# Attention stage of a fused kernel: conversion steps moved between GpSimd and VectorE, expert weights loaded over more steps

## The chip, the cores and the metric

One core of a Trainium2 chip runs the whole program. The metric is the device time of one execution in microseconds; lower is better.

## The reference

Three layers follow one another: a linear attention with decay, a soft mixture of experts, and an ELU feed-forward. Cut to what matters:

```python
for t in range(S):                                   # attention: B=4, H=8, S=768, D=48
    cur = einsum('bhd,bhe->bhde', u * k[t], v[t])
    y[t] = einsum('bhd,bhde->bhe', r[t], state + cur)
    state = w * state + einsum('bhd,bhe->bhde', k[t], v[t])
logits = x @ phi                                     # soft MoE: 3072 tokens, 384 wide, 8 experts x 4 slots
d = softmax over tokens;  c = softmax over slots
slot_out[e] = relu((d.T @ x)[e] @ w1[e]) @ w2[e]     # w1: 384 x 1024, w2: 1024 x 384
x = c @ slot_out
h = x @ w_in                                         # ELU layer, 384 -> 2048 -> 384
out = where(h > 0, h, exp(min(h, 0)) - 1) @ w_out
```

The weights `w_in` and `w_out` of the last layer arrive as 64-bit floating-point numbers, and the kernel converts them to 32 bits with integer and float instructions.

## The kernel before, in words

The program has three stages: attention (to about 175 us), the experts, and the feed-forward. The change touches attention alone.

**Attention.** The 3072 tokens are cut into 24 chunks of 128 (4 batches of 6 chunks). One loop, `for s in range(-2, NCH)`, runs over them as a pipeline: step s finishes chunk s, computes the scores of chunk s + 1 and transposes r and k of chunk s + 2. Every engine executes its instructions in the order in which this loop writes them, so the order of the calls in the loop body is the schedule. In one step VectorE has: `t` (state, line 582), `km` (k times decay, line 517), `x` (output of the chunk, line 635), two `am` (causal masks on the scores, line 559), `rT` (scaling of the transposed r, line 532) and `qd` (r x k, line 529). TensorE has the state update, the rows of the output, the scores, and the transposes: `ps_r` of r, `ps_k` of k. The transposes share two PSUM buffers, so `ps_k` waits until `rT` has read `ps_r`. ScalarE copies `ps_k` to `kT` (line 527) and the state to `qb` (line 589). GpSimd multiplies the state by its decay (`qc`, line 583) and v by the bonus (`bv`, line 601). Between these stand, through `extra()`, the instructions of the experts' softmax over groups of three chunks (`al`, `nmx`, `et`, `pall`, `zr`): each three steps bring each of them once.

**Conversion.** 20 pieces of 128 x 384 numbers of `w_in` and `w_out` are converted during attention, one in each of the steps 0 to 19. `wide(j, f)` performs one part of it on piece j; all work in the tile `scr`:

- `wide_a`, ScalarE, lines 313 and 314: absolute value of the high word; the low word as a float.
- `wide_b1`, line 317, the clamp: limits the absolute value to the range of exponents. In attention it is given `nc.gpsimd`, so GpSimd does it.
- `wide_b2`, VectorE, line 322, the shift: shift left by 3 and a bit mask.
- `wide_b3`, VectorE, line 328, the merge: sign and top bits of the high word are put in.
- `wide_c`, VectorE, line 333, the mask: keeps sign and exponent.
- `wide_d`, GpSimd, lines 336 and 337, the product of the low word and the scale, and the sum; it is done one step later, for piece s - 1.

The raw data of three pieces and the working words of two fit in `scr`, so `wide_load(s + 2)` waits for `wide_d` of piece s - 1. The second stage of this conversion, in the feed-forward, calls the same functions with the clamp on VectorE.

**Loads.** SyncE issues all large loads in order: r, k and v of the chunks ahead, a piece for the conversion, and the experts' weights (`load_we`, 1.5 MB a set, 16 sets) into ten buffers, one of which holds `scr` until the last piece is done. Sets 0 to 8 are issued at the ends of steps by a rule that spreads them, set 9 when `scr` is free, set 10 in two halves in steps 21 and 22.

Of the kernel before, what the change touches and what calls it, by code (L numbers as in the profile page):

```python
# [236 lines left out]
def kernel(  # L237
# [14 lines left out]
    nc = tc.nc  # L252
# [25 lines left out]
    NWE = 10  # L278
    we_p = main.enter_context(tc.tile_pool(name="we_p", bufs=NWE, side="right"))
# [33 lines left out]
        nc.scalar.activation(out=a.bitcast(F32), in_=raw[:, :, 1].bitcast(F32), func=ACTF.Abs)  # L313
        nc.scalar.activation(out=l.bitcast(F32), in_=l.bitcast(U32), func=ACTF.Copy, scale=2.0 ** -52)

    def wide_b1(raw, a, eng=None):
        (eng or nc.vector).tensor_scalar(  # L317
            out=a.bitcast(F32), in0=a.bitcast(F32), scalar1=EXP_LO, scalar2=EXP_HI, op0=ALU.max, op1=ALU.min
        )

# [31 lines left out]
    def load_we(i, pool, part=None):  # L352
        if part in (None, 0):
            t = pool.tile([128, 2 * HW], F32, tag="we", name=f"we{i}")
            we[i] = [t[:, :HW], t[:, HW:]]
        for h in range(2) if part is None else [part]:
            load_half(i, h)

    def load_half(i, h):
        n = FE if i < E else DM  # L360
        src = (w1[i] if i < E else w2[i - E]).rearrange("(k p) f -> p k f", p=128)
        at = 0
        while at < HW:
            k, c = divmod(HW * h + at, n)
            m = min(HW - at, n - c)
            if c == 0 and m == n:
                m = (HW - at) // n
                nc.sync.dma_start(
                    out=we[i][h][:, at:at + n * m].rearrange("p (k f) -> p k f", k=m), in_=src[:, k:k + m]
                )  # L370
                at += n * m
            else:
                nc.sync.dma_start(out=we[i][h][:, at:at + m], in_=src[:, k, c:c + m])
                at += m
# [22 lines left out]
    with ExitStack() as actx:  # L397
# [22 lines left out]
        def warm(n):  # L420
            ps = pt_p.tile([128, 4, 128], F32, tag="pt", name="warm")
            for i in range(n):
                nc.tensor.matmul(out=ps[:, i % 4, :], lhsT=ident, rhs=ident, start=True, stop=True)
# [95 lines left out]
        def turn(i, n):  # L519
            ps = pt_p.tile([128, HP, 128], F32, tag="pt", name=f"ps_{'rk'[i]}")  # L520
            for p in range(HP):
                nc.tensor.transpose(  # L522
                    out=ps[:, p, :], in_=(km if i else rp[n % 2])[:, 2 * p:2 * p + 2, :].rearrange("p a d -> p (a d)"),
                    identity=ident,
                )
            if i:
                nc.scalar.copy(out=kT, in_=ps)  # L527
                qd[n] = at2.tile([128, HP, 128], F32, tag="qd", name="qd", bufs=1)
                nc.vector.tensor_tensor(out=qd[n], in0=rT[n], in1=ps, op=ALU.mult)
            else:  # L530
                rT[n] = at2.tile([128, HP, 128], F32, tag="rT", name="rT", bufs=2)
                nc.vector.tensor_tensor(out=rT[n], in0=ps, in1=vt, op=ALU.mult)  # L532
# [58 lines left out]
        def bonus_b(n):  # L591
            bt = misc.pop(n)
            pb = pm_p.tile([128, 128], F32, tag="pm", name="ps_c")
            nc.tensor.transpose(out=pb, in_=bt, identity=ident)
            bs = at2.tile([128, H], F32, tag="bs", name="bs", bufs=1)
            nc.scalar.copy(
                out=bs.rearrange("p (a b) -> p a b", b=2),
                in_=pb.rearrange("p (a b) -> p a b", b=32)[:, :, 0:2],
            )
            bv = at2.tile([128, H, D], F32, tag="bv", name="bv", bufs=1)  # L600
            nc.gpsimd.tensor_tensor(out=bv, in0=vd[n], in1=bs.unsqueeze(2).to_broadcast([128, H, D]), op=ALU.mult)  # L601
            bsb[n] = bv
# [79 lines left out]
        def slots_b(j):  # L682
            el, ps, nj = lg[j], lg[j, 0], nmx[:, j:j + 1]
            nc.scalar.activation(out=el[:, 0, :], in_=ps[:96], func=ACTF.Exp, bias=nj, accum_out=zz[:, j:j + 1])
            if j:
                nc.scalar.activation(out=wt[j], in_=nmx[:, j - 1:j], func=ACTF.Exp, scale=-1.0, bias=nj)
# [54 lines left out]
        def last_part(j):  # L741
            slots_a(j, False)
            slots_b(j)
            combine_a()
            warm(4)
            extra()
            slots_c(j, (0,))
            warm(2)
            slots_d(j, (0,))
            slots_g(j)  # L750
            combine_c()
            slots_e(j)
            slots_f(j)
            slots_c(j, (1,))
            warm(2)
            combine_b()
            slots_d(j, (1,))
# [25 lines left out]
        NP = -(-NW // PW)  # L783
# [29 lines left out]
        def wide(j, f):  # L813
            if 0 <= j < NP:
                raw, a = piece(j)
                if f is wide_b1:
                    f(raw, a, nc.gpsimd)
                    return
                if f is not wide_d:
                    f(raw, a)  # L820
                    return
                merged = []
                for o, at, i, c, p, m in spans(j):
                    if merged and merged[-1][0] == o:
                        merged[-1][3] += m
                    else:
                        merged.append([o, at, p, m])
                for o, at, p, m in merged:
                    wide_d(raw[:, at:at + m, :], a[:, at:at + m], (wov if o else wiv)[:, p:p + m])
# [18 lines left out]
        nwe = 0  # L848
        extras = [lambda: None] * 7 + [flags_a, lambda: None, lambda: None, flags_b, lambda: None, flags_c, flags_d]

        def extra():
            if extras:
                extras.pop(0)()
# [3 lines left out]
        for s in range(-2, NCH):  # L857
            now, nxt, ahead = s >= 0, 0 <= s + 1 < NCH, s + 2 < NCH
            last = s == NCH - 1
            if nxt:  # L860
                update(s + 1)
            wide(s, wide_a)
            wide(s, wide_b1)
            if last:
                extra()
                extra()
                extra()
                logits(GS - 1, 0, G - 1)
            else:
                extra()  # L870
            if s > 0 and s % G == 0:
                extras += part(s // G - 1)
            if s == -2:
                tables_b()
            if nxt:
                state(s + 1)
            if ahead:
                scale(s + 2)
            if 2 <= s + 4 < NCH:
                load_k(s + 4)  # L880
            if 2 <= s + 3 < NCH:
                load_v(s + 3)
            if s < 1:
                wide_load(s + 2)
            if now:
                for p in range(HP):
                    rows_a(s, p)
                rows_b(s)
                wide(s, wide_b2)
                wide(s - 1, wide_d)  # L890
                if s >= 1 and s + 2 < NP:
                    wide_load(s + 2)
            if nxt:
                for p in range(HP):
                    scores(s + 1, p)
                causal(s + 1)
                bonus_a(s + 1)
                bonus_c(s + 1)
            if not last:
                extra()  # L900
            if ahead:
                turn(0, s + 2)
            if 2 <= s + 4 < NCH:
                load_r(s + 4)
            if nxt:
                for p in range(HP):
                    before(s + 1, p)
            if now:
                x_T(s)
            if last:  # L910
                logits(GS - 1, G - 1, G)
            if nxt:
                bonus_b(s + 1)
            wide(s, wide_b3)
            wide(s, wide_c)
            if ahead:
                turn(1, s + 2)
            if nxt:
                state_b(s + 1)
            if s == NCH - 2:  # L920
                warm(3)
            extra()
            if s >= 2 and (s - 2) * (NWE - 1) // (NP - 3) >= nwe and nwe < NWE - 1:
                load_we(nwe, we_p)
                nwe += 1
            if s == NP:
                assert nwe == NWE - 1
                load_we(nwe, we_p)
                nwe += 1
            if s >= NCH - 3 and not last:  # L930
                h = s - NCH + 3
                (rk_ctx, early)[h].close()
                pool = w2ctx.enter_context(tc.tile_pool(name=f"we2a{h}", bufs=1, side="right", reuse_waits="tile"))
                we.setdefault(NWE, []).append(pool.tile([128, HW], F32, name=f"we2a{h}"))
                load_half(NWE, h)
                nwe = NWE + h
        last_part(GS - 1)
        assert not extras

# [464 lines left out]
```

## Time and profile before

| | us |
|---|---|
| three runs | 466.58, 467.81, 467.82 |
| median | 467.81 |
| the profiled execution | 467.28 |
| its span, first to last instruction | 465.5 |
| TensorE busy | 416.9 (90% of the span) |
| VectorE busy | 369.6 (79%) |
| ScalarE busy | 268.5 (58%) |
| GpSimd busy | 186.3 (40%) |

The time of an execution holds a little more than its span. Busy times are sums over the whole span, in which the three stages have different limits; the attention stage is read from its own stretch.

### The profile page before, as it was taken

Reading aid. Unit: us, or ns where it says so; the run is one execution under the profiler, and the core shown is the slowest. Engines: PE = TensorE matmul, PEld = TensorE weight load, DVE = VectorE, ACT = ScalarE, POOL = GpSimd, SP = SyncE. Lnnn points to the kernel's source line nnn. Section 1 sums busy time; section 2 is a strip of 40 time slices with the busy share of each in tenths; the row PEclk is TensorE's granted clock in tenths of the full one; section 3 lists DMA queues with packets and bytes.
Section 4 is the critical chain, followed back from the end, with each engine's and each line's share of the span. In section 5 each row is a group of like instructions: output and inputs, shape, how many; then the busy total and the mean of one; then the engine's idle time right before and its main releaser. Section 6 shows DMA issues by size and latency. Waiting matters only on the chain.

```text
span 465.5 us, 9991 instructions
## 1 busy us (share of the span) xinstructions
PE 416.9 (90%) x4009; PEld 365.4 (78%) x4009; DVE 369.6 (79%) x553; ACT 268.5 (58%) x487; POOL 186.3 (40%) x185
## 2 busy tenths in 40 slices
PE   7888788798879898995999899989999999999995
PEld 6777677676768774443899789969998989999994
DVE  4798889898988854454887999996999987787851
ACT  2444254345445332485677787867868686866740
POOL 2385667777777613200000245331234304324440
PEclk9999899999999999998899999999999999999999
DMA  9959989999999858850000111211111001111112
GB/s 127 214 124 273 232 211 252 259 281 261 277 233 244 228 200 271 294 182 0 2 1 0 34 35 35 67 36 35 34 35 34 1 0 51 36 52 68 70 70 73
DMA packets 97575, 57.41 MB, mean 123 GB/s; under 512 B 77808, under 2 KB 89328, under 8 KB 97520
## 3 DMA queue, kind: packets, MB, share of 16 engines
q1 hardware_dynamic: 96704, 56.64, 45.2%
q8 instruction: 33, 0.54, 0.5%
q14 instruction: 22, 0.18, 0.1%
q10 hardware_dynamic: 816, 0.05, 0.1%
HBM read 51.96 MB, written 4.72 MB: 122 GB/s over the span
## 4 chain that ended last, share of the span: by engine, by line
PE 50%; DVE 16%; POOL 13%; ACT 10%; issue 8%; DMA 3%; POOLq 0%; DVEq 0%; ACTq 0%; SPq 0%
PE fo L1256 12%; PE fo L1257 11%; PE fo L1259 11%; POOL scr L317 5%; PE fh L1211 3%; DVE ex L1230 3%; DVE ex L1225 3%; DMA scr<-in_moe_w_out_dram 2%; POOL scr L336 2%; PE ph L1011 2%; POOL bv L601 2%; DVE am L559 2%; ACT scr L313 1%; PE ps_a L554 1%; ACT th L1219 1%
## 5 line engine op out<-in xcount | busy, mean ns | idle before, releaser
L1256 PE MATMUL fo<-wh,gh 128*128 128x384 f32 x384 | 132.3, 344 | 7.0 <-ACT gh L1238 3.7
L1257 PE MATMUL fo<-wl,gh 128*128 128x384 f32 x384 | 130.7, 340 | 0.0
L1259 PE MATMUL fo<-wh,gl 128*128 128x384 f32 x384 | 122.2, 340 | 0.0
L1256 PEld LDWEIGHTS fo<-wh,gh 128*128 128x128 f32 x384 | 72.9, 190 | 14.0 <-ACT acc L1193 6.5
L1225 DVE SCALAR_TENSOR_TENSOR ex<-ex,th 128x1024 f32<-128x1024 f32 (+1 forms) x52 | 62.1, 1195 | 23.3 <-ACT ex L1222 23.1
L336 POOL TENSOR_TENSOR cv<-raw,cv 128x384 f32<-128x384 f32 x12 | 19.8, 1652 | 138.7 <-DVE cv L333 66.4
L1241 DVE TENSOR_TENSOR gl<-ex,gh 128x1024 fp32r<-128x1024 f32 (+1 forms) x52 | 72.0, 1385 | 3.5 <-ACT gh L1238 3.0
L1219 ACT ACTIVATE th<-fh 128x1024 f32<-128x1024 f32 (+1 forms) x53 | 50.3, 949 | 42.4 <-PE fh L1211 42.4
L1257 PEld LDWEIGHTS fo<-wl,gh 128*128 128x128 f32 x384 | 72.8, 190 | 1.9
L1259 PEld LDWEIGHTS fo<-wh,gl 128*128 128x128 f32 x384 | 72.2, 190 | 0.0
L1230 DVE SCALAR_TENSOR_TENSOR ex<-ex,fh 128x1024 f32<-128x1024 f32 (+1 forms) x52 | 58.8, 1131 | 0.1
L1222 ACT ACTIVATE ex<-fh 128x1024 f32<-128x1024 f32 (+1 forms) x53 | 50.3, 949 | 9.5 <-DVE gl L1241 9.4
L1238 ACT CAST gh<-ex 128x1024 fp32r<-128x1024 f32 (+1 forms) x52 | 51.5, 991 | 5.4 <-DVE ex L1230 4.2
L1198 POOL TENSOR_TENSOR acc<-os,acc 128x384 f32<-128x384 f32 x20 | 29.0, 1482 | 49.7 <-ACT os L1197 49.7
L317 POOL TENSOR_SCALAR scr<-scr 128x384 f32<-128x384 f32 x20 | 30.8, 1538 | 35.7 <-ACT scr L313 35.7
L522 PE MATMUL ps_k<-ident,km 128*128 128x128 f32 x96 | 15.9, 290 | 23.5 <-DVE rT L532 22.2
L646 ACT COPY xT<-ps_x 128x384 f32<-128x384 f32 x24 | 11.5, 479 | 38.6 <-PE ps_x L644 38.6
L1211 PE MATMUL fh<-cT,mst 128*128 128x512 f32 x96 | 31.0, 404 | 2.8 <-DVE ex L1230 2.8
L522 PEld LDWEIGHTS ps_k<-ident,km 128*128 128x128 f32 x96 | 10.4, 143 | 28.4 <-DVE rT L532 26.7
L527 ACT COPY kT<-ps_k 128x512 f32<-128x512 f32 x24 | 14.1, 587 | 30.4 <-PE ps_k L522 30.2
L559 DVE TENSOR_TENSOR am<-ps_a,mask 128x512 f32<-128x512 f32 x48 | 30.7, 678 | 0.9 <-PE ps_a L554 0.9
L554 PE MATMUL ps_a<-rT,kT 64*128 64x128 f32 x384 | 29.0, 292 | 0.6 <-DVE rT L532 0.6
(160 smaller groups left out, 729.0 us busy)
## 6 DMA issues: line engine op xcount, KB each, us to landing
we<-in_moe_w_dram SPq DMA_DIRECT2D x14, 768.0 KB, 7.6
we<-in_moe_w_dram SPq DMA_DIRECT2D x16, 512.0 KB, 6.4
rp<-in_r_dram SPq DMA_DIRECT2D x24, 192.0 KB, 4.7
rk<-in_k_dram SPq DMA_DIRECT2D x24, 192.0 KB, 4.9
vd<-in_v_dram SPq DMA_DIRECT2D x24, 192.0 KB, 5.2
out_dram<-acc SPq DMA_DIRECT2D x24, 192.0 KB, 1.9
we<-in_moe_w_dram SPq DMA_DIRECT2D x16, 256.0 KB, 6.0
scr<-in_moe_w_out_dram SPq DMA_DIRECT2D x10, 384.0 KB, 5.1
```

Source lines behind the costliest of these rows:

```text
L317: (eng or nc.vector).tensor_scalar(out=a.bitcast(F32), in0=a.bitcast(F32), scalar1=EXP_LO, scalar2=EXP_HI, op0=ALU.max, op1=ALU.min)
L559: nc.vector.tensor_tensor(out=am[n, a], in0=aps[a], in1=mask.unsqueeze(1).to_broadcast([128, HP, 128]), op=ALU.mult)
L1211: nc.tensor.matmul(out=ph[n][:, i, :], lhsT=mst[(f + i) // 8][:, 128 * ((f + i) % 8):128 * ((f + i) % 8) + 128], rhs=cT[:, TB * blk:TB * b ...
L1219: nc.scalar.activation(out=th[n][:, s], in_=ph[n][:, s], func=ACTF.Tanh, scale=0.5)
L1222: nc.scalar.activation(out=ex[n][:, s], in_=ph[n][:, s], func=ACTF.Exp)
L1225: nc.vector.scalar_tensor_tensor(out=ex[n][:, s], in0=ex[n][:, s], scalar=1.0, in1=th[n][:, s], op0=ALU.add, op1=ALU.mult)
L1230: nc.vector.scalar_tensor_tensor(out=ex[n][:, s], in0=ex[n][:, s], scalar=0.0, in1=ph[n][:, s], op0=ALU.min, op1=ALU.max)
L1238: nc.scalar.copy(out=gh[n][:, s], in_=ex[n][:, s])
L1241: nc.vector.tensor_tensor(out=gl[n][:, s], in0=ex[n][:, s], in1=gh[n][:, s].bitcast(F32), op=ALU.subtract)
L1256: nc.tensor.matmul(out=o, lhsT=gh[n][:, i, s], rhs=wh, start=(f == first), stop=False)
L1257: nc.tensor.matmul(out=o, lhsT=gh[n][:, i, s], rhs=wl, start=False, stop=False)
L1259: nc.tensor.matmul(out=o, lhsT=gl[n][:, i, s], rhs=wh, start=False, stop=(f == final))
```

## The change

1. The clamp is no longer called right behind `wide_a` for GpSimd. It stands on VectorE behind `rows_b` (that is, behind `x` and ahead of `am`), where the shift stood.
2. The shift stands behind `bonus_b` and ahead of `turn(1, ...)`, that is on VectorE between `rT` and `qd`.
3. Merge and mask stand behind `turn(1, ...)`, that is behind `qd`.
4. Sets 0 to 8 of the experts' weights are spread by `(s - 2) * 9 // 20` instead of `// 17`: they are issued at the ends of steps 2, 5, 7, 9, 11, 14, 16, 18 and 20 instead of 2, 4, 6, 8, 10, 12, 14, 16 and 18; set 9 in step 21 instead of 20.

```diff
-    def wide_b1(raw, a, eng=None):
-        (eng or nc.vector).tensor_scalar(
+    def wide_b1(raw, a):
+        nc.vector.tensor_scalar(
...
         def wide(j, f):
             if 0 <= j < NP:
                 raw, a = piece(j)
-                if f is wide_b1:
-                    f(raw, a, nc.gpsimd)
-                    return
...
             wide(s, wide_a)
-            wide(s, wide_b1)
...
                 rows_b(s)
-                wide(s, wide_b2)
+                wide(s, wide_b1)
                 wide(s - 1, wide_d)
...
             if nxt:
                 bonus_b(s + 1)
+            wide(s, wide_b2)
+            if ahead:
+                turn(1, s + 2)
             wide(s, wide_b3)
             wide(s, wide_c)
-            if ahead:
-                turn(1, s + 2)
...
-            if s >= 2 and (s - 2) * (NWE - 1) // (NP - 3) >= nwe and nwe < NWE - 1:
+            if s >= 2 and (s - 2) * (NWE - 1) // NP >= nwe and nwe < NWE - 1:
                 load_we(nwe, we_p)
                 nwe += 1
-            if s == NP:
-                assert nwe == NWE - 1
-                load_we(nwe, we_p)
-                nwe += 1
+            if s == NP + 1:
+                load_we(NWE - 1, we_p)
```

VectorE before, one step from rT to rT (`scr` is the conversion's tile; lines 322, 328 and 333 are shift, merge and mask):

```order
L532 TENSOR_TENSOR rT<-ps_r,vt 128x512
L328 SCALAR_TENSOR_TENSOR scr<-scr 128x384
L333 TENSOR_SCALAR scr<-scr 128x384
L529 TENSOR_TENSOR qd<-rT,ps_k 128x512
L669 TENSOR_REDUCE al<-ps_l 96x1
L670 TENSOR_SCALAR nmx<-al,nmx 96x1
L582 TENSOR_TENSOR t_149<-qc,pu 128x192
L517 TENSOR_TENSOR km<-rk_835,wk 128x8x48
L635 TENSOR_TENSOR x<-py,bv 128x384
L322 TENSOR_SCALAR scr<-scr 128x384
L559 TENSOR_TENSOR am<-ps_a,mask 128x512 x2
L532 TENSOR_TENSOR rT<-ps_r,vt 128x512
```

Merge and mask (lines 328 and 333) stand together between rT and qd, the shift (line 322) alone ahead of am.

VectorE in the same step of the change:

```order
L532 TENSOR_TENSOR rT<-ps_r,vt 128x512
L322 TENSOR_SCALAR scr<-scr 128x384
L529 TENSOR_TENSOR qd<-rT,ps_k 128x512
L328 SCALAR_TENSOR_TENSOR scr<-scr 128x384
L333 TENSOR_SCALAR scr<-scr 128x384
L669 TENSOR_REDUCE al<-ps_l 96x1
L670 TENSOR_SCALAR nmx<-al,nmx 96x1
L582 TENSOR_TENSOR t_149<-qc,pu 128x192
L517 TENSOR_TENSOR km<-rk_829,wk 128x8x48
L635 TENSOR_TENSOR x<-py,bv 128x384
L317 TENSOR_SCALAR scr<-scr 128x384
L559 TENSOR_TENSOR am<-ps_a,mask 128x512 x2
```

Between rT and qd there is now one conversion instruction (the shift) instead of two, behind qd there are two instead of none, and ahead of am the clamp (line 317) has the shift's place.

GpSimd before, one step and the start of the next:

```order
L317 TENSOR_SCALAR scr<-scr 128x384
L583 TENSOR_TENSOR qc<-t_149,w_141 128x192
L336 TENSOR_TENSOR scr<-scr 128x384
L337 TENSOR_TENSOR win<-scr 128x384
L601 TENSOR_TENSOR bv<-vd,bs 128x384
L317 TENSOR_SCALAR scr<-scr 128x384
```

Each step begins with the clamp (line 317), ahead of qc.

GpSimd in the change, the same place:

```order
L583 TENSOR_TENSOR qc<-t_149,w_141 128x192
L336 TENSOR_TENSOR scr<-scr 128x384
L337 TENSOR_TENSOR win<-scr 128x384
L601 TENSOR_TENSOR bv<-vd,bs 128x384
L583 TENSOR_TENSOR qc<-t_149,w_141 128x192
```

The clamp at the head of each step is gone, and qc follows bv directly.

## Rows read from the trace of the kernel before

The view by stretches (rows 1) has these columns: stretch, its length, busy us (and instructions) of TensorE's matmuls, its weight loads, VectorE, ScalarE and GpSimd; then granted clock, DMA share and GB/s. The views in order of time have the start in us, the duration in us, engine, line, operation, output and inputs, shapes, and in brackets the idle time before and what ended it.

**Rows 1.** Busy us of each engine, TensorE's granted clock, DMA share, GB/s, by stretches.
```profile
41.40:152.60 111.20, 92.88 (x1578) 78.43 (x1578) 97.75 (x184) 51.86 (x152) 79.25 (x77) 0.98 1.00 253
161.00:168.00 7.00, 7.00 (x140) 6.40 (x137) 5.45 (x13) 2.77 (x9) 1.52 (x2) 1.00 1.06 380
168.00:175.00 7.00, 5.83 (x88) 4.68 (x85) 3.01 (x7) 1.69 (x7) 0.83 (x1) 1.00 0.17 60
49.00:56.00 7.00, 6.11 (x87) 5.07 (x88) 5.81 (x12) 2.00 (x5) 4.66 (x5) 0.76 0.79 215
```

**Rows 2.** VectorE in order of time (start, us): the first and last rT.
```profile
41.40 0.68 DVE L532 TENSOR_TENSOR rT<-ps_r,vt 128x512 f32<-128x512 f32 x1
...
152.62 0.67 DVE L532 TENSOR_TENSOR rT<-ps_r,vt 128x512 f32<-128x512 f32 x1
```

**Rows 3.** VectorE in order of time, one step (in brackets: idle before, released by).
```profile
111.45 0.68 DVE L532 TENSOR_TENSOR rT<-ps_r,vt 128x512 f32<-128x512 f32 x1
112.05 0.66 DVE L328 SCALAR_TENSOR_TENSOR scr<-scr 128x384 int32<-128x384 int32 x1
112.75 0.87 DVE L333 TENSOR_SCALAR scr<-scr 128x384 int32<-128x384 int32 x1
113.55 0.69 DVE L529 TENSOR_TENSOR qd<-rT,ps_k 128x512 f32<-128x512 f32 x1
114.16 0.25 DVE L700 COPY et<-ps_e 128x96 f32<-128x96 f32 x1
114.32 0.35 DVE L582 TENSOR_TENSOR t<-qc,pu 128x192 f32<-128x192 f32 x1
...
115.05 0.55 DVE L635 TENSOR_TENSOR x<-py,bv 128x384 f32<-128x384 f32 x1
116.52 0.66 DVE L322 TENSOR_SCALAR scr<-scr 128x384 int32<-128x384 int32 x1 [0.91 <-POOL scr L317]
117.09 1.28 DVE L559 TENSOR_TENSOR am<-ps_a,mask 128x512 f32<-128x512 f32 x2
118.29 0.68 DVE L532 TENSOR_TENSOR rT<-ps_r,vt 128x512 f32<-128x512 f32 x1
```

**Rows 4.** GpSimd (POOL) in order of time, the same step.
```profile
112.26 1.14 POOL L601 TENSOR_TENSOR bv<-vd,bs 128x384 f32<-128x384 f32 x1
114.79 1.69 POOL L317 TENSOR_SCALAR scr<-scr 128x384 f32<-128x384 f32 x1 [1.39 <-ACT scr L313]
116.45 0.50 POOL L583 TENSOR_TENSOR qc<-t,w 128x192 f32<-128x192 f32 x1
```

**Rows 5.** VectorE in order of time, qd in a step without a piece.
```profile
160.72 0.69 DVE L529 TENSOR_TENSOR qd<-rT,ps_k 128x512 f32<-128x512 f32 x1 [1.72 <-ACT kT L527]
```

**Rows 6.** Lines 317 and 333: ns min/median/max, first and last start.
```profile
L317 DVE TENSOR_SCALAR cv<-cv x12: 347/348/356, 252.3 to 364.4; 128x384 f32<-128x384 f32 x12
L333 DVE TENSOR_SCALAR scr<-scr x20: 360/869/872, 21.4 to 153.9; 128x384 int32<-128x384 int32 x20
```

**Rows 7.** GpSimd and VectorE in order of time, near 89.3 us.
```profile
89.24 1.02 POOL L336 TENSOR_TENSOR scr<-scr 128x384 f32<-128x384 f32 x1
...
89.31 1.17 DVE L322 TENSOR_SCALAR scr<-scr 128x384 int32<-128x384 int32 x1 [1.31 <-POOL scr L317]
```

**Rows 8.** VectorE and GpSimd in order of time, the step behind the last piece.
```profile
155.49 0.35 DVE L582 TENSOR_TENSOR t<-qc,pu 128x192 f32<-128x192 f32 x1
...
155.98 0.69 POOL L583 TENSOR_TENSOR qc<-t,w 128x192 f32<-128x192 f32 x1 [1.42 <-ACT c_sb L702]
...
156.63 1.02 POOL L336 TENSOR_TENSOR scr<-scr 128x384 f32<-128x384 f32 x1
156.72 0.69 DVE L559 TENSOR_TENSOR am<-ps_a,mask 128x512 f32<-128x512 f32 x1
```

**Rows 9.** VectorE in order of time: softmax instructions ahead of t in another step.
```profile
121.00 0.61 DVE L720 SCALAR_TENSOR_TENSOR pall<-pall,al,ps_s 96x384 f32<-96x384 f32 x1
...
121.65 0.34 DVE L582 TENSOR_TENSOR t<-qc,pu 128x192 f32<-128x192 f32 x1
```

More of the change, by code (lines that the diff above doesn't have):

```diff
@@ L936 @@
                 nwe = NWE + h
+        assert nwe == NWE + 1
         last_part(GS - 1)
```

## Prediction, made before the changed kernel was run

> **What bounds the kernel now.** I read the busy time by stretches first, then VectorE's and GpSimd's instructions of one step in order of time, then the places where one of them waits.
>
> Of the 111.2 us in which 16 of the 20 pieces are converted, VectorE is busy for 97.75, TensorE for 92.88, GpSimd for 79.25 [rows 1]. No engine is full, so the stretch is a ring of waits. One turn of it is one step, from r's scaling (rT) to the next rT: 41.40 to 152.62 for 16 steps [rows 2], 111.22 us, 6.95 us a step.
>
> A step [rows 3, 4]: rT starts at 111.45. It lets TensorE transpose k, ScalarE copies the result (kT) and VectorE's r x k (qd) waits for that copy: where nothing lies between, qd sat idle for 1.72 us and the releaser is kT [rows 5]. In a step with a piece qd starts 2.10 us after rT (113.55 - 111.45), and that time is filled exactly by the merge (line 328) and the mask (line 333). Then ScalarE takes the absolute value of the next piece, GpSimd's clamp waits for it and runs from 114.79 for 1.69 us, and VectorE's shift (line 322) waits 0.91 us for the clamp [rows 3, 4]. Behind the shift stand the two causal masks (am) and the next rT. So the ring is rT, k's transpose, kT, ScalarE, clamp, shift, am, rT, and the slow clamp is on it.
>
> **The change part by part.**
>
> *The clamp leaves GpSimd.* It goes from the ring, with the 0.91 us wait: a gain. GpSimd then has only qc, the product and the sum (lines 336 and 337) and bv in a step.
>
> *The clamp on VectorE, between x and am.* Undisturbed this instruction takes 0.35 us on VectorE: the second stage has twelve of them, 347 to 356 ns [rows 6]. But the one-input integer instructions on VectorE that run beside GpSimd here do not keep their 0.36 us (the mask's minimum); the mask's median is 0.87 [rows 6]. The row that explains it: GpSimd's product starts at 89.24 and lasts 1.02 us, VectorE's shift starts 0.07 us later and lasts 1.17, until 0.22 us after the product's end [rows 7]. The mask does the same beside bv: bv ends at 113.40, the mask at 113.62 [rows 3, 4]. So such an instruction that finds a GpSimd product running waits for its end.
>
> The Trainium skill says why, in "SBUF — State Buffer", section "SBUF: two separate sides": VectorE in a two-port mode and GpSimd share a port pair, whoever starts first holds it for the whole instruction, and the other blocks. By that rule too the clamp costs either its bare time or the rest of a GpSimd instruction, and who starts first decides; the 1.17 us row agrees.
>
> Who starts first? In the step where the last piece's products run and no clamp is left [rows 8], t starts at 155.49, qc on GpSimd at 155.98 and the product at 156.63, that is 1.14 us behind t; the instruction behind x on VectorE (there am) starts at 156.72, 1.23 us behind t. The clamp will stand in that place. It comes 0.09 us after the product, nearly the 0.07 us of the blocked shift [rows 7]. So I take 1.17 us and not 0.35. Successors start some 0.08 us before an instruction ends (rT lasts 0.68, the merge starts 0.60 behind it [rows 3]), so the clamp delays am by 1.09 us blocked, 0.30 us free. These are the two ends.
>
> *The shift into the gap behind rT.* It takes 0.36 us free, 0.66 as it stood [rows 3], or until 0.22 us behind bv's end; all of it lies in the 2.10 us before qd. Cost nothing; if bv came 1 us later than now, qd would slip.
>
> *Merge and mask behind qd.* They leave a gap which now stays partly empty and come onto VectorE's line: 0.60 us for the merge (0.70 beside bv as it stands [rows 3], the upper end; bv will be over) and 0.30 for the mask. The mask's bounds are 0.36 and 0.87 us [rows 6]; it comes some 3.3 us after rT, and bv, which began 0.81 us after rT and took 1.14 [rows 3, 4], is through by then, so the lower. Who waits for the mask: the product, which stands behind qc anyway.
>
> *The sum of a step.* rT to qd 2.10, qd to the next 0.61, merge 0.60, mask 0.30; then the softmax instructions e; t to clamp 1.23; clamp 1.09; the two am 1.20 (118.29 - 117.09) [rows 3]: 7.13 + e. e is 0.16 in one step of three (et, 114.16 to 114.32 [rows 3]), 0.65 in the next (pall to t, 121.00 to 121.65 [rows 9]), and I put the third kind between, 0.40, an estimate; mean 0.40. That is 7.53 us against 6.95. VectorE alone is then the ring: it has no wait but the one for kT. TensorE, busy 92.88 of 111.2 us at these steps, has room.
>
> Sixteen steps: +0.58 x 16 = +9.3; three of them have no t, a 0.26 us shorter line, -0.8. Of the four steps before, three at +0.5; the first has no product on GpSimd yet, its clamp is free and the wait is gone, -0.6. The step behind the last piece has merge and mask on the line, no clamp: +0.5. Sum +9.9.
>
> *Experts' weights over 20 steps.* Each set is loaded up to three steps later, the last at step 21 instead of 20. Loads get thinner in the piece steps, where 253 GB/s flow; no wait of the ring names a load there, so I count no gain. At the end about one set (1.5 MB) more lies behind step 20: at 380 GB/s some 4.1 us [rows 1], an estimate. The 7 us after it move 60 GB/s at a share of 0.17, so 5.8 us are free. Zero; if that cover were gone, up to 4 us.
>
> 467.28 us (the profiled execution; its span is 465.5) + 9.9 = **477.2 us**. That execution lies 0.53 us under the median of the three runs, 467.81, closer than the sum is sure.
>
> **The rivals.**
>
> *The clamp comes first (faster).* If it starts before the product, it costs 0.30 us and the product waits. A step is then 6.34 + 0.40 = 6.74: 13 steps at -0.21 are -2.7. In the three without t the products run earlier, the clamp meets the second one, and they stay near 7.27: +0.9. Three earlier steps -0.6, the first -0.6, the last +0.5: -2.5, **464.8 us**. For it: the margin is 0.09 us, read off starts, and the instruction in that place, an am, takes no part in the blocking [rows 8]. Against it: the shift was blocked at 0.07 [rows 7]. The point that decides is whether the product starts less than 1.23 us behind t. By the rule of the Trainium skill's "SBUF — State Buffer" (the section above) nothing but this order decides, and the one case at hand, [rows 7], went as it says.
>
> *In some steps first, in some not (no change).* Each free clamp saves 0.79 us, so some 11 or 12 of the 16 to 17 blocked ones must come free to end within the bound of no change: about 468. The steps repeat to 0.02 us in the trace, which speaks against a mixture.
>
> *TensorE's clock falls (slower still).* TensorE's work per step stays, the step grows, so it idles more. Once in the kernel before, after the long step that began at 41.40, the granted clock fell: 0.76 over 49 to 56 us, part of it at 1.2 GHz instead of 2.4 [rows 1]. That is 7 x 0.24 = 1.7 us of full-speed time for one fall. Three more falls not covered by its idle time give +5: **482 us**. Against it: other long steps went by at 1.00, the 111.2 us hold 0.98 in the mean.
>
> **How the numbers follow.** Forecast 477.2 us with a chance of 0.63 (474 to 480, from the bounds of merge, mask and e); clamp first 464.8, 0.21; mixture 468, 0.07; clock 482, 0.09. The range from 464.0 to 482.0 takes in the forecast, the mixture, over half of the fast rival and about half of the clock rival; the likeliest case alone is 474 to 480. Within 0.3% (1.4 us, about what a measurement of this kernel can tell from no change) only part of the mixture and the edge of the fast rival lie: 0.06. Faster 0.22, slower 0.72.
>
> **What would show it.** Right: line 317 on VectorE at about 1.17 us, ending 0.2 us behind the product of line 336; qd with some 1 us idle time released by kT in every piece step; the wait of the shift for the clamp gone; GpSimd's busy time down by about 30 us; rT to rT 7.2 to 7.8 us. Wrong: a clamp of 0.35 us in most steps (then the fast rival), a shift that ends after kT (then qd slips and the step is longer than the sum), or steps short of 6.9 us whose end a load or TensorE sets. Attention's end should move by all of the difference, and the stages behind it by nothing.

## The result, and the profile after

| | before | change |
|---|---|---|
| runs (4 each), us | 466.57 to 467.82 | 460.32 to 462.08 |
| median, us | 467.19 | 460.93 |
| ratio, 95% interval | | 0.9872 [0.9844, 0.9899] |
| profiled execution, us | 467.28 | 460.49 |

The change is faster by 6.3 us. The prediction said slower, 477.2 us, and its range began at 464. The page of the changed kernel, parts 1 and 4 (busy us, share of the span, instructions; shares of the chain that ended last):

```profile
span 458.8 us, 10035 instructions
...
PE 416.3 (91%) x4009; PEld 360.9 (79%) x4009; DVE 369.1 (80%) x573; ACT 267.9 (58%) x487; POOL 156.6 (34%) x165
...
PE 57%; DVE 22%; ACT 10%; issue 8%; DMA 2%; POOL 1%; SPq 0%; DVEq 0%; ACTq 0%; POOLq 0%
```

Part 4 of before:

```profile
PE 50%; DVE 16%; POOL 13%; ACT 10%; issue 8%; DMA 3%; POOLq 0%; DVEq 0%; ACTq 0%; SPq 0%
```

GpSimd lost 29.7 us of work and has almost left the chain, where VectorE and TensorE took its place. The busy times of TensorE, VectorE and ScalarE are those of before within 1 us. The view by stretches (columns as in [rows 1]) for the same 16 steps, whose first and last rT [rows 2] now start at 38.50 and 146.50:

```profile
38.50:146.50 108.00, 94.81 (x1578) 77.08 (x1578) 98.29 (x200) 51.32 (x150) 56.92 (x61) 1.00 0.98 250
```

108.0 us, against 111.2 of before [rows 1] and 119.7 of the forecast (13 steps of 7.53, three of 7.27). Attention's start gained too: 29.3 us from the first rT to 38.50, where before took 32.2. VectorE of the change in order of time, one step and the next up to qd (columns as in [rows 3]):

```profile
98.20 0.68 DVE L532 TENSOR_TENSOR rT<-ps_r,vt 128x512 f32<-128x512 f32 x1
98.80 0.47 DVE L322 TENSOR_SCALAR scr<-scr 128x384 int32<-128x384 int32 x1
100.30 0.69 DVE L529 TENSOR_TENSOR qd<-rT,ps_k 128x512 f32<-128x512 f32 x1 [1.03 <-ACT kT L527]
100.91 0.55 DVE L328 SCALAR_TENSOR_TENSOR scr<-scr 128x384 int32<-128x384 int32 x1
101.49 0.36 DVE L333 TENSOR_SCALAR scr<-scr 128x384 int32<-128x384 int32 x1
...
102.22 0.34 DVE L582 TENSOR_TENSOR t<-qc,pu 128x192 f32<-128x192 f32 x1
...
103.41 1.17 DVE L317 TENSOR_SCALAR scr<-scr 128x384 f32<-128x384 f32 x1
104.50 1.27 DVE L559 TENSOR_TENSOR am<-ps_a,mask 128x512 f32<-128x512 f32 x2
105.70 0.67 DVE L532 TENSOR_TENSOR rT<-ps_r,vt 128x512 f32<-128x512 f32 x1
106.30 0.47 DVE L322 TENSOR_SCALAR scr<-scr 128x384 int32<-128x384 int32 x1
107.00 0.69 DVE L529 TENSOR_TENSOR qd<-rT,ps_k 128x512 f32<-128x512 f32 x1 [0.23 <-ACT kT L527]
```

The first step is the forecast in the flesh: qd 2.10 us behind rT with 1 us of idle time, the clamp blocked for 1.17 us, the mask at 0.36, and 7.50 us from rT to rT where the sum said 7.53. The second is not: its qd starts 1.30 us behind rT, and it takes 6.44 us. TensorE in order of time says why (k's transposition in those two steps):

```profile
98.93 0.66 PE L522 MATMUL ps_k<-ident,km 128*128 128x128 f32 x4 [0.43 <-DVE rT L532]
...
105.64 0.66 PE L522 MATMUL ps_k<-ident,km 128*128 128x128 f32 x4 [0.46 <-ACT xT L646]
```

In the first step it waits for rT and starts 0.73 us behind rT's start. In the second it waits for ScalarE's copy xT of the transposed output, and starts 0.06 us ahead of rT. The view of waits (us in total, times, longest; 10 to 180 us), before:

```profile
PE ps_k L522 <- DVE rT L532: 22.2, 19, 2.3
...
PE ps_k L522 <- ACT xT L646: 0.5, 1, 0.5
```

and the change:

```profile
PE ps_k L522 <- ACT xT L646: 6.4, 14, 0.5
PE ps_k L522 <- DVE rT L532: 5.2, 6, 1.3
```

Three tiles share the two PSUM buffers of one pool: `ps_r`, `ps_k` and `ps_x` (the transposed output). So `ps_k` does not always wait until `rT` has read `ps_r`, as the words on the kernel before have it. Which buffer `ps_k` gets is picked when the program is built; by what rule, no run shows. The code of `turn`, which asks for it, is the same in both kernels. Where it gets the buffer that `ps_r` has just held, it waits for rT; where it gets that of `ps_x`, for xT. In TensorE's instructions this is one word, before first, then the change, for the same chunk:

```
L522 MATMUL ps_k_1129<-ident_71,km_145 128x128 [waits DVE_49]
L522 MATMUL ps_k_1122<-ident_71,km_145 128x128 [waits Activation_49]
```

Over the 24 chunks, with D for a wait on VectorE's rT and A for one on ScalarE's xT, before has one A, the change DDDAADAAAADAAADADAAAADDD: 14 A. (In both kernels the first two chunks wait for neither; they are written D here.) In the first two runs below, the moves with the old loads have ten A and before with the new loads has one. So the moves themselves changed the pick, and behind them the loads changed it once more.

### The profile page after: what moved, and what is told of

It is laid out like the page before. It is cut to its first block, busy times and chain, and to the rows that moved or that the text cites. A ratio compares the mean times of both kernels' runs of the same rounds, so it can differ in the third digit from the quotient of the medians.

```text
span 458.8 us, 10035 instructions
## 1 busy us (share of the span) xinstructions
PE 416.3 (91%) x4009; PEld 360.9 (79%) x4009; DVE 369.1 (80%) x573; ACT 267.9 (58%) x487; POOL 156.6 (34%) x165
## 4 chain that ended last, share of the span: by engine, by line
PE 57%; DVE 22%; ACT 10%; issue 8%; DMA 2%; POOL 1%; SPq 0%; DVEq 0%; ACTq 0%; POOLq 0%
PE fo L1252 12%; PE fo L1255 11%; PE fo L1253 11%; PE fh L1207 3%; DVE ex L1226 3%; DVE ex L1221 3%; PE py L612 3%; PE ps_k L522 3%; PE ps_a L554 2%; DVE am L559 2%; PE ph L1007 2%; PE py L625 2%; DVE scr L317 2%; DVE km L517 2%; ACT th L1215 1%
## 5 line engine op out<-in xcount | busy, mean ns | idle before, releaser
L583 POOL TENSOR_TENSOR qc<-t,w 128x192 f32<-128x192 f32 x20 | 14.5, 724 | 59.7 <-DVE t L582 21.8
L529 DVE TENSOR_TENSOR qd<-rT,ps_k 128x512 f32<-128x512 f32 x24 | 16.4, 685 | 15.4 <-ACT kT L527 15.4
L554 PE MATMUL ps_a<-rT,kT 64*128 64x128 f32 x384 | 27.9, 285 | 0.3 <-ACT kT L527 0.2
L625 PE MATMUL py<-vd,am 128*64 128x48 f32 x768 | 26.5, 222 | 0.0
```

The costliest lines, as they stand in the source:

```text
L554: nc.tensor.matmul(out=aps[a][:, p, :], lhsT=kT[q, p, :], rhs=rT[n][q, p, :], start=True, stop=True)
```

## The experiments

Three explanations stood against each other: the **wait** (k's transposition freed from rT, in 14 chunks), the **loads** (issued over 20 steps), and the **moves** themselves (a clamp on VectorE that costs less than the sum held). "Before" in a run below is timed beside it on the same chip.

**The loads alone, both ways.** The change with the old load lines:

```diff
-            if s >= 2 and (s - 2) * (NWE - 1) // NP >= nwe and nwe < NWE - 1:
+            if s >= 2 and (s - 2) * (NWE - 1) // (NP - 3) >= nwe and nwe < NWE - 1:
...
-            if s == NP + 1:
-                load_we(NWE - 1, we_p)
+            if s == NP:
+                assert nwe == NWE - 1
+                load_we(nwe, we_p)
+                nwe += 1
```

> The change, with the expert weights spread as before (sets 0 to 8 by // 17, set 9 in step 20). Theory A (the gain comes from the order of VectorE and GpSimd and from the PSUM buffer that k's transposition gets): 461 us, within 1 us of the change. Theory C (a part of the gain comes from the thinner loads): at least 2 us slower than the change, 463 to 467 us.

465.44 us, ratio 0.9967 [0.994, 0.9994]: 4.5 us slower than the change. It looks like the loads, but the waits moved too: five later chunks went back from A to D. Two of them open pairs of steps of 7.07 and 8.49 us, 5.64 and 7.50 in the change; in the 8.49 us k waits for a late xT, and TensorE's clock fell once in each pair, at 94 and 139 us. So this run alone decides nothing. Before with the new load lines:

> The kernel before, with the expert weights spread over 20 steps and nothing else. Theory A: 467 us, within 1 us of before. Theory C: 461 to 465 us.

466.43 us, ratio 1.0006 [0.9969, 1.0042]: in before, the new loads bring nothing. Its profiled execution shows something else. The view by stretches, before:

```profile
8.00:13.00 5.00, 4.18 (x42) 3.55 (x40) 2.58 (x5) 1.06 (x2) 0.74 (x1) 0.66 0.98 174
49.00:54.00 5.00, 4.11 (x62) 3.82 (x64) 3.81 (x10) 1.73 (x4) 2.93 (x4) 0.66 0.72 170
```

and this run:

```profile
8.00:13.00 5.00, 4.00 (x57) 3.15 (x56) 3.41 (x7) 1.33 (x3) 0.74 (x1) 1.00 0.99 177
49.00:54.00 5.00, 4.99 (x91) 3.83 (x89) 4.41 (x11) 2.10 (x6) 3.41 (x4) 1.00 0.67 159
```

Twice before's TensorE ran partly at 1.2 GHz (granted clock 0.66) where this execution kept 2.4. The first fall makes the first two steps 11.03 instead of 9.75 us, the second one step 7.17 instead of 5.91: 2.5 us that come and go between executions: before itself, timed beside this run, has five executions at the same granted clock as this one (0.990 in the mean), with spans of 462.6 to 462.9 us. Against a fall-free span of 462.7 the change gains 3.9 us.

**The wait alone, both ways.** The change with `ps_k` fixed to the buffer of `ps_r`, all 24 chunks D:

```diff
-        pt_p = actx.enter_context(tc.tile_pool(name="pt_p", bufs=2, space=PSUM))
+        pt_p = actx.enter_context(tc.tile_pool(name="pt_p", bufs=1, space=PSUM))
...
-            ps = pt_p.tile([128, HP, 128], F32, tag="pt", name=f"ps_{'rk'[i]}")
+            ps = pt_p.tile([128, HP, 128], F32, tag="pta" if i else "pta", name=f"ps_{'rk'[i]}")
...
-            ps = pt_p.tile([128, KD, 128], F32, tag="pt", name="ps_x")
+            ps = pt_p.tile([128, KD, 128], F32, tag="ptb", name="ps_x")
```

> The change, with two PSUM tiles of fixed use: r's and k's transposition share one, x's has the other, so k's transposition waits for rT in all steps, as it does in 19 of 22 piece steps of before. Theory A: qd starts 2.1 us behind rT in all steps, a step takes the 7.5 us of my sum where the clamp is blocked and 6.7 where not; 469 to 477 us. Theory B (the buffer does not matter; the gain is the slow clamp that left the ring): 461 us, within 1.5 us of the change.

474.5 us, ratio 1.0163 [1.0105, 1.0222]. Nothing was changed but the buffers, and the kernel is 13.6 us slower than the change. Of this, 1.8 us lie in the first two steps, whose k waits for rT in neither before nor the change. Its waits, 10 to 180 us:

```profile
DVE qd L529 <- ACT kT L527: 27.5, 24, 1.6
...
PE ps_k L522 <- DVE rT L532: 20.5, 18, 2.6
```

qd comes at least 2.09 us behind rT in every step. The 16 steps take 115.9 us, with three falls of the clock among them and one ahead that the change does not have. That 474.5 us comes close to the 477.2 forecast is in part luck: the falls are in it, and its 16 steps are 3.8 us short of the forecast's 119.7. Before with `ps_k` in the buffer of `ps_x`, all A (the same edit with "ptb" for k):

> The kernel before, with fixed PSUM tiles the other way: x's and k's transposition share one, so k's transposition waits for ScalarE's copy of x's and no longer for rT. Theory A: kT, the absolute value, the clamp and the shift come earlier in those steps where xT was done long before rT (up to 1.3 us in some); 460 to 465 us with the clamp still on GpSimd. Theory B: 467 us, within 1 us of before.

461.61 us, ratio 0.9892 [0.9843, 0.9942]. The kernel before, with no instruction moved, gains as much as the change did; its 16 steps take 105.8 us. Its profiled execution has no fall in attention: the span is 459.3 us, 3.4 below the fall-free 462.7. The change with all A (as there, 22 of the 24 chunks):

> The change with k's transposition in x's PSUM tile in all steps (22 of 24 chunks; 14 in the change). Theory A: qd comes 0.9 to 2.1 us behind rT in all steps, 455 to 460 us. If k then waits too long for xT, since x stands behind merge and mask on VectorE: 461 to 466 us.

460.8 us, ratio 0.9905 [0.9881, 0.9929]: no better than 14 A. The 16 steps are 1.8 us shorter, but the start is 0.9 us longer and what follows them 1.2 us.

**Loads and buffers held apart.** The order of buffers of the change written out as a table, first in the change with old loads, then in before:

```diff
+        SEQ = "DDDAADAAAADAAADADAAAADDD"
...
+            if i == 0:
+                r0 = "ptb" if bank[1] == "pta" else "pta"
+                bank[0], bank[2] = r0, "ptb" if r0 == "pta" else "pta"
+                bank[1] = r0 if SEQ[n] == "D" else bank[2]
+            ps = pt_p.tile([128, HP, 128], F32, tag=bank[i], name=f"ps_{'rk'[i]}")
```

> The change with the weights spread as before, and with each transposition put by hand into the PSUM tile that it has in the change (k's in x's tile in 14 of 24 chunks, in r's tile in 10). Theory A (the load rule counted only because it moved k's transposition to r's tile in five later chunks): 461 us, within 1.5 us of the change. Theory C (the loads themselves cost): 464 to 466 us, as in the run with the old loads and free tiles.

> The kernel before, with each transposition put by hand into the PSUM tile that it has in the change. Theory A: most of the change's gain without any of its moves, between the run with k behind xT throughout and before: 462 to 464 us. If the moves on VectorE and GpSimd carry the gain: 466 to 467 us.

465.29 us, ratio 0.9971 [0.9951, 0.999], and 465.48 us, ratio 0.9978 [0.9952, 1.0003]. Both are blurred by a fault of the edit: my table made the first `ps_r` wait, and the first two steps took 12.0 us (with a fall of the clock) and 11.6, not 8.45 as in the change. Behind them the steps of the first run equal the change's. With the first entries of the table mended:

> The change with the old spread of the weights and the PSUM tiles of the change put by hand, now from the first chunk on (in the run before this one the first transposition of r had to wait for the copy of another tile, and the first two steps took 12.0 us against 8.4). Theory A: 461 us, within 1 us of the change; every step as in the change. Theory C (loads): 464 to 466 us.

> The kernel before with the PSUM tiles of the change, mended at the start in the same way. In the 16 steps the first try took 107.0 us against 109.9 of before without a clock fall. Theory A: 462.5 to 464.5 us. If the start was not the reason: 465.5 us again.

463.88 us, ratio 0.9962 [0.9942, 0.9982], and 464.5 us, ratio 0.9974 [0.9936, 1.0012]. The first is a miss (461 us was expected), yet every step from the third on repeats the change's within 0.04 us with the old loads. Its start is still 1.8 us longer than the change's, all of it in the first two steps: the table's D makes k wait for rT there (qd 2.1 us behind rT in both; 1.51 and 0.87 in the change, where k waits for neither). Another 1.4 us lies behind the last rT, where the profiled executions of all these kernels scatter by 2.0. So the loads by themselves are worth 1.4 us at most, and that much is not shown. In the second, before's 16 steps with the change's buffers take 105.7 us; before with the new loads, without a fall, had 109.9. Again the start (the two D, and a clock fall at 10 to 14 us) took back part of what the steps gave.

**The clamp, alone and elsewhere.** Before with only the clamp moved to VectorE, ahead of the shift:

```diff
-                if f is wide_b1:
-                    f(raw, a, nc.gpsimd)
-                    return
...
-            wide(s, wide_b1)
...
+                wide(s, wide_b1)
                 wide(s, wide_b2)
```

> The kernel before, with the clamp alone moved to VectorE, right ahead of the shift; shift, merge, mask and loads as before; k's transposition waits for rT in nearly all steps. Theory A with the lock of the products: the clamp is blocked as in the change, the shift behind it, 0.3 to 0.7 us a step more than before: 470 to 476 us. Theory B (the slow clamp off the ring is the gain): 461 to 465 us.

472.59 us, ratio 1.0126 [1.0101, 1.015]: as expected. VectorE of this run in order of time:

```profile
109.92 1.17 DVE L317 TENSOR_SCALAR scr<-scr 128x384 f32<-128x384 f32 x1
111.13 1.06 DVE L322 TENSOR_SCALAR scr<-scr 128x384 int32<-128x384 int32 x1
```

The clamp is blocked by the product, then the shift by the sum. That is what moving the shift behind rT spares the change. The clamp at the head of the step, right behind `wide_a`, to make it free:

```diff
             wide(s, wide_a)
+            wide(s, wide_b1)
...
-                wide(s, wide_b1)
```

> The change, with the clamp on VectorE at the head of the step, ahead of t, where GpSimd has no product running. The wait for GpSimd's product goes (11 of 20 clamps took 1.17 us in the change), each saves 0.8 us on VectorE's line. If VectorE's line sets the step: 453 to 457 us. If something else does (TensorE, the loads): 459 to 461 us.

481.39 us, ratio 1.0312 [1.0285, 1.0339], a clear miss. VectorE in order of time, then one stretch of the run:

```profile
119.74 0.69 DVE L529 TENSOR_TENSOR qd<-rT,ps_k 128x512 f32<-128x512 f32 x1 [2.38 <-ACT kT L527]
...
121.21 0.35 DVE L317 TENSOR_SCALAR scr<-scr 128x384 f32<-128x384 f32 x1
```

```profile
92.00:100.00 8.00, 7.64 (x89) 6.81 (x92) 4.92 (x13) 2.28 (x6) 1.92 (x3) 0.57 0.69 185
```

The clamp is free, but it stands ahead of x, so x, its transposition and xT come later, and k's transposition waits for xT in most chunks; qd started 2.1 to 3.8 us behind rT, and TensorE fell to 1.2 GHz in five long stretches and a short one. The same with all chunks D:

> The change with the clamp at the head of the step (VectorE, no product beside it) and k's transposition behind rT in all steps. This is the sum of the prediction with a free clamp: 2.10 + 0.61 + 0.60 + 0.30 + 0.27 + 0.40 + 1.23 + 1.20 = 7.6 less the 0.9 us that the blocked clamp would have cost, 6.7 us a step: 463 to 466 us, where the same tiles with the blocked clamp gave 474.5. If the blocked clamp was not what made those steps long: 472 to 476 us.

475.14 us, ratio 1.0222 [1.0172, 1.0271]. VectorE in order of time:

```profile
91.44 0.36 DVE L317 TENSOR_SCALAR scr<-scr 128x384 f32<-128x384 f32 x1 [0.67 <-ACT scr L313]
91.71 1.37 DVE L517 TENSOR_TENSOR km<-rk,wk 128x384 f32<-128x384 f32 x1
```

A free clamp is not free here: in every third step it waits for ScalarE's absolute value, and in three of these km (0.55 us alone) runs into GpSimd's sum. Four falls of the clock lie in its 16 steps as well. The price of a step with a free clamp in my fast rival, 6.74 us, was not reached as a mean in any run of this kind.

**k ahead of rT.** If the wait for rT costs that much, it can go altogether: k's transposition right behind r's, in a buffer of its own, r and x sharing the other. In the change:

```diff
+            wide(s, wide_b2)
+            if ahead:
+                turn(1, s + 2)
...
-            wide(s, wide_b2)
-            if ahead:
-                turn(1, s + 2)
```

> The change, with k's transposition right behind r's on TensorE and in a tile of its own (r and x share the other): it waits neither for rT nor for xT, so kT is done before the shift is, and qd has no idle time. If these waits are the cause: VectorE's line is am 1.20, rT 0.60, shift 0.30, qd 0.60, merge 0.60, mask 0.30, e 0.40, t to clamp 1.23, clamp 0.3 to 1.09: 5.5 to 6.3 us a step against 6.75, 450 to 456 us. If not (the blocked clamp or TensorE sets the step): 459 to 462 us.

458.39 us, ratio 0.981 [0.9791, 0.9829]: the best version, its interval below the change's, but between the two ranges that were expected. VectorE in order of time, then GpSimd's bv of that step:

```profile
72.09 0.68 DVE L532 TENSOR_TENSOR rT<-ps_r,vt 128x512 f32<-128x512 f32 x1
72.69 0.34 DVE L322 TENSOR_SCALAR scr<-scr 128x384 int32<-128x384 int32 x1
72.95 0.67 DVE L529 TENSOR_TENSOR qd<-rT,ps_k 128x512 f32<-128x512 f32 x1
...
74.13 0.94 DVE L333 TENSOR_SCALAR scr<-scr 128x384 int32<-128x384 int32 x1
...
78.32 0.67 DVE L532 TENSOR_TENSOR rT<-ps_r,vt 128x512 f32<-128x512 f32 x1
```

```profile
74.03 0.83 POOL L601 TENSOR_TENSOR bv<-vd,bs 128x384 f32<-128x384 f32 x1 [2.17 <-ACT bs L596]
```

qd starts 0.86 us behind rT with no idle time, and the 16 steps take 6.10 to 6.91 us each. Part of the gain goes into a new wait: the mask, now earlier, begins 0.10 us behind bv and takes 0.94 instead of 0.36 us. Before with the same edit:

> The kernel before with the same tiles and place of k's transposition. kT no longer waits for rT, so the absolute value, the clamp on GpSimd and the shift come earlier; merge and mask stand between rT and qd as before. If the waits for the tile are the cause: 454 to 460 us with no move of clamp, shift, merge or mask. If not: 464 to 467 us.

465.39 us, ratio 0.9963 [0.9927, 1.0]. VectorE in order of time:

```profile
105.34 0.66 DVE L322 TENSOR_SCALAR scr<-scr 128x384 int32<-128x384 int32 x1 [1.05 <-POOL scr L317]
```

There the shift still waits for GpSimd's clamp, and the 16 steps take 107.8 us, against 104.3 of the run above (which has the new loads too). So in these runs moving the clamp off GpSimd is worth something only where k's wait is out of the way. Last, the best version with product and sum behind bv, so that the clamp meets neither:

```diff
-                wide(s - 1, wide_d)
...
+            wide(s - 1, wide_d)
```

> The first of these three with GpSimd's product and sum behind bv instead of ahead of it, so that VectorE's clamp meets only qc, which ends before it. If the blocking is by the product alone: line 317 takes 0.35 us in nearly all steps, steps near 5.7 us where TensorE's own work sets them, 446 to 452 us. If the products then block shift or mask instead, or bv comes late: 452 to 462 us.

479.05 us, ratio 1.025 [1.0233, 1.0267], a clear miss. GpSimd, ScalarE and VectorE, in order of time:

```profile
98.40 1.21 POOL L337 TENSOR_TENSOR win<-scr 128x384 f32<-128x384 f32 x1
...
99.65 0.56 ACT L313 ACTIVATE scr<-scr 128x384 f32<-128x384 f32 x1 [3.32 <-POOL win L337]
...
100.24 0.36 DVE L317 TENSOR_SCALAR scr<-scr 128x384 f32<-128x384 f32 x1 [1.03 <-ACT scr L313]
```

The clamp takes 0.36 us, but the working words of only two pieces exist, so ScalarE's absolute value of a new piece waits for the late sum, and the clamp for ScalarE.

## Why the prediction was wrong

**The step that failed** is the first term of the sum: "rT to qd 2.10", taken from "In a step with a piece qd starts 2.10 us after rT". That is true of all 16 of before's steps (2.10 or 2.11 us). But the prediction took for granted that rT is what k's transposition waits for. In before 19 of 20 such waits name rT; it is the pick of a buffer, and the moves changed it. In the change qd comes 0.87 us behind rT in three of the 16 steps, 1.30 in two, 1.75 to 1.77 in three and 2.09 to 2.13 in eight (four of which are A with a late xT): 1.71 in the mean. That is 0.39 us a step less than 2.10, 6.2 us of the 11.7 by which the 16 steps undercut the forecast. The run with all D (474.5 us) and before with all A (461.61) show that this wait turns the sign. The prediction compared the order of instructions on VectorE and GpSimd, where nothing tells of this wait, and not the waits on TensorE.

The sign of the moves themselves was forecast rightly for k's wait as before has it. At equal buffers they make the 16 steps longer: from 109.9 to 115.9 us with k behind rT (three falls of the clock in the second figure), from 105.7 to 108.0 with the change's buffers, from 105.8 to 106.2 with all A. They make them shorter, 107.8 to 104.3, only with k ahead of rT. (The loads differ too in three of these pairs; held apart, they brought these steps nothing.)

**The clamp was right in most steps, and mis-sized in the others.** 1.17 to 1.18 us in 11 of 20 pieces; 0.64 to 0.70 in three; 0.34 or 0.35 in six. Of the 16 steps, five have a free one (0.8 us less each, 4.0) and three, those without t, a half-blocked one (0.5 less each, 1.5), another 5.5 us: with the 6.2 above this closes the gap of 11.7. The mixture, which I gave 0.07 because steps repeat, is what happened: the free ones come every three steps. All five stand in the steps with pall. GpSimd of the change there, then VectorE's clamp:

```profile
96.02 0.80 POOL L583 TENSOR_TENSOR qc<-t,w 128x192 f32<-128x192 f32 x1 [2.92 <-DVE t L582]
96.78 1.18 POOL L336 TENSOR_TENSOR scr<-scr 128x384 f32<-128x384 f32 x1
```

```profile
96.74 0.35 DVE L317 TENSOR_SCALAR scr<-scr 128x384 f32<-128x384 f32 x1
```

The multiplication qc lasted 0.80 us instead of 0.69, so the product came 0.04 us behind the clamp rather than 0.06 ahead of it. So it is in four of the five. The fifth goes against the order of the starts (GpSimd, then VectorE):

```profile
55.90 1.28 POOL L336 TENSOR_TENSOR scr<-scr 128x384 f32<-128x384 f32 x1
...
55.96 0.35 DVE L317 TENSOR_SCALAR scr<-scr 128x384 f32<-128x384 f32 x1
```

There the product started 0.06 us ahead by the profile, as beside the blocked clamps, and yet the clamp was free and the product took 1.28 us. "The point that decides", as the prediction put it, fits 19 of the 20 clamps; what it lacked was that the margin of 0.09 us does not hold in all steps. Why qc lasts longer in the four, and why the fifth clamp was free, stays open. The Trainium skill's "SBUF — State Buffer", section "SBUF: two separate sides", has whoever starts first hold the shared ports for its whole instruction. Apart from that fifth clamp the rows agree in both directions: the blocked clamp of 103.41 us ended 0.22 us behind the product, and behind the free clamp the product took 1.18 instead of 1.02 us.

**The start of attention** was forecast at +0.9 us up to 38.50 and came at -2.9. Of this, 1.3 us is the clock fall of before; the step of the first piece gained 1.3 us, not 0.6; the other three steps together gained 0.3 us where the forecast had them lose 1.5 (one that turned to A gained 0.8, the two others lost 0.4 and 0.1).

**Right:** GpSimd's busy time down by about 30 us (29.7), the mask at 0.36 us, the shift hidden between rT and qd (0.34 to 0.94 us, no qd slipped), the loads by themselves at about nothing, the step behind the last piece (0.43 us longer, forecast 0.5), attention as the place of nearly all of the difference (its last rT comes 6.0 us earlier, of 6.7 between the two spans), and the sum itself: 7.50 to 7.53 us in the steps where qd was late and the clamp blocked.

**The clock** went the other way in the change than the rival said; in the run with all D, where the steps did grow, it fell as the rival had it. A fall-free span of 462.7 puts the effect of the change at 3.9 us; the other 2.4 us of the median's 6.3 are about what before's two falls cost (2.5), and the change shows none in attention. In the profiled executions falls in attention were many where the 16 steps were longest (six with the clamp at the head, with the clamp alone moved and with the products last, five with the clamp at the head and all D, four with all D) and few elsewhere: none in the change, in both kernels with all A and in before with k ahead of rT. But before with the new loads, k behind rT nearly throughout, had none either. That is a pattern over these runs, not a cause that was isolated.

## What to carry to other kernels

After instructions are moved, compare the waits of every engine and not only the order: tiles that share a pool can trade buffers, and that was worth more here than the change that was meant. Fix the buffers before judging a move. An instruction freed of one wait meets the next one (the mask and bv in the best version), and one moved to a place where it is cheap can make its input or its successors late, as three of these runs show.

## What was not expected of the hardware

A few hundredths of a microsecond between two engines go with 0.8 us: a clamp 0.06 us behind the start of GpSimd's product took 1.17 us (once only 0.35), one 0.04 us ahead of it 0.35. And km, a product of two SBUF operands that takes 0.55 us alone, took 1.37 us when it began 0.21 us behind GpSimd's sum. Beside GpSimd's clamp it lost far less: in before, a km that began 0.27 us behind such a clamp of 1.54 us (80.75 and 80.48 us) took 0.70 us and ended 0.57 us ahead of the clamp's end.
